# One planned order for attention and experts: other planned landing times for transfers, and one due-time shift per operation

## The chip, the cores and the metric

The kernel runs on one core of a Trainium2 chip. The metric is the device time of one execution in microseconds (us), less is better. TensorE is called PE here, VectorE DVE, ScalarE ACT, GpSimd POOL and SyncE SP. Each engine works through its own list of instructions in the order in which the program issued them; an instruction that waits holds up everything behind it on its engine.

## The reference, cut to what matters

```python
scores = scale * q @ k.T                       # 8 batches x 8 heads, 576 x 576, head size 64
thresh = max(scores, axis=-1) - tau
scores = where(scores >= thresh, scores, -1e9)
attn = softmax(scores);  x = attn @ v          # x as 4608 tokens x 512
e_idx = argmax(x @ w_gate + modality_bias[modality_id])      # one of 8 experts per token
h = relu(x[mask] @ w1[e]);  out[mask] = gate_w * (h @ w2[e]) # 512 -> 1024 -> 512
```

## The kernel before

**Attention** goes through 32 pairs of heads (4 pairs to a batch) with 9 steps each, 288 steps in all. A step is: scores on PE (line 819, into one of two score buffers `s`), negated row maximum on DVE (828), exponential on ACT (834), mask and sum on DVE (846, into `pr`), four transposes of `pr` on PE (872) and their copy on ACT (875). The rest of each score row goes through `rp` (copied on POOL in the first 54 steps, line 859; transposed on PE at 885 and 889). After a pair come the products with v (753, `ptm` and `ptr`). Ahead of a pair its q and k rows are loaded into the single buffer `kq` by SP (line 482), transposed on PE (684 and 690), copied on ACT, and split by POOL into `q` (719, 721), from which SP copies `km`, `nk` and `q` halves.

**Experts.** When a batch's four pairs are done, `gate` (966, 976) and `route` work out each token's expert and place: the transposes at 976, a chain on DVE that ends in `oh` (1009), the counting matmuls on `oh` (printed with line 753), again DVE, and five scatters into the table `tab` (POOL, 1038). Eight side slots, one for each batch, take up to 512 routed tokens each: SP reads the slot's list `tb` from `tab` (1156), POOL gathers its tokens' rows `xg` (1165), PE transposes them (1182), weights come through `raw` (1198, 1203) and are split by POOL (1216, 1218), PE computes both layers (1234 and 1266) with ACT and DVE between them (1246 `hh`, 1248 `hl`), and POOL scatters the result (1285). What is left is worked out by `pick_rest` on DVE (from 1065) after the last attention step and done in a tail.

**What sets the order.** Nothing is issued as written: each `op(...)` is recorded with a cost and a due time, and `Plan.order` plays the program through with these costs, always starting the waiting operation that is due first on a free engine. A transfer is given an issue time, a share of a common transfer queue and a landing time; a consumer is not placed before its input has landed in this play. The order that comes out is fixed at build time. Where the play leaves PE free for over 0.6, `Plan.fill` puts small matmuls of zeros there (line 1430, here called fillers), which do nothing but keep PE at work. Before the play each operation's due time is shifted: in the kernel before by some 900 entries `(seed, lo, hi, wide)`, each of which adds Gaussian noise of width `wide` to all operations due between `lo` and `hi`.

Of the kernel before, what the change touches and what calls it, by code (L numbers as in the profile page):

```python
# [76 lines left out]
class Plan:  # L77
# [65 lines left out]
    def order(self, banks, late):  # L143
# [43 lines left out]
        dma = [0.0]  # L187
# [10 lines left out]
        def begin(e, t):  # L198
# [3 lines left out]
            for j in coming:  # L202
                x = ops[j]
# [35 lines left out]
            if o.dma is not None:  # L239
                s = max(dma[0], end + (0.9 if t > self.COLD else 0.0))  # L240
                dma[0] = s + 1.15 * o.dma
                fin = dma[0] + (2.6 if t > self.COLD else 1.2)
                if e == "POOL":
                    fin = max(fin, end + 3.7)
                    sent.append(fin)
            else:
                fin = end
# [94 lines left out]
def tile_attn_moe(  # L342
# [19 lines left out]
    N = B * S  # L362
# [1066 lines left out]
    def idle(g, n):  # L1429
# [3 lines left out]
    SHIFTS = [  # L1433
# [180 lines left out]
```

## Time and profile before

| | us |
|---|---|
| median of 3 runs | 1006.26 (1003.15 to 1007.72) |
| profiled execution | 999.88 |
| its span, from the first instruction to the last | 998.1 |
| PE busy in the span | 969.2 (97%) |
| DVE busy | 738.6 (74%) |
| ACT busy | 616.6 (62%) |
| POOL busy | 562.8 (56%) |
| mean granted clock of PE | 0.996 of full |

The profiled execution lies 6.4 us below the median of the runs, and 1.8 us of it lie outside the span. Busy time is the union of an engine's instructions; PE's matmuls overlap, and a filler counts as busy.

### The profile page before, as it was taken

To read this page: it belongs to the slowest core of one execution; us is meant where nothing else is said; L and a number is where in the kernel's file an instruction comes from. 1 tells how busy PE (TensorE), PEld (TensorE's weight loads), DVE (VectorE), ACT (ScalarE), POOL (GpSimd) and SP (SyncE) were. 2 spreads that over 40 slices of the span, in tenths; PEclk is the share of its full clock that TensorE was granted. 3 is DMA by queue.
4 is the path that set the end of the run, shared out by engine and by line. 5 is a ranking of instruction groups with operands and counts; after the bars stand their busy time and mean duration, and the time that the engine had idled before them with its cause. 6 is when DMAs were issued, how large, how long until landed. Compare 5 with 4: busy or idle time off the path is not lost.

```text
span 998.1 us, 20124 instructions
## 1 busy us (share of the span) xinstructions
PE 969.2 (97%) x6527; PEld 782.4 (78%) x6527; DVE 738.6 (74%) x1802; ACT 616.6 (62%) x1256; POOL 562.8 (56%) x693
## 2 busy tenths in 40 slices
PE   7989989999999999999999999999999999999997
PEld 6667678777888877888888778877887778888886
DVE  7889878898888888888988888878886373233341
ACT  6677667777777767777677667765775213243431
POOL 5433577475557652756666564646854679933341
PEclk9999999999999999999999999999999999999999
DMA  8787798789969975789689786987662258443421
GB/s 173 132 188 176 159 191 197 157 175 192 187 121 196 208 185 101 161 183 210 159 160 238 168 179 100 211 170 165 142 178 86 66 149 265 137 125 102 121 81 40
DMA packets 291122, 158.10 MB, mean 158 GB/s; under 512 B 199038, under 2 KB 262526, under 8 KB 289088
## 3 DMA queue, kind: packets, MB, share of 16 engines
q1 hardware_dynamic: 281696, 137.28, 63.0%
q0 software_dynamic: 7200, 18.92, 6.3%
q8 instruction: 54, 0.88, 0.4%
q10 hardware_dynamic: 2112, 0.52, 0.3%
q14 instruction: 60, 0.49, 0.2%
HBM read 85.83 MB, written 19.35 MB: 105 GB/s over the span
## 4 chain that ended last, share of the span: by engine, by line
PE 85%; DVE 5%; issue 3%; DMA 3%; ACT 1%; POOL 1%; SPq 0%; DVEq 0%; POOLq 0%; ACTq 0%
PE s L819 16%; PE bk L1266 16%; PE bk L753 15%; PE bk L1234 14%; PE bk L872 11%; PE pm L1234 3%; PE pm L1266 2%; PE bk L1182 1%; PE bk L941 1%; PE bk L885 1%; DMA tab<-pay,posi 1%; PE bk L966 1%; DVE nm L828 1%; DVE pr L846 1%; ACT e L834 1%
## 5 line engine op out<-in xcount | busy, mean ns | idle before, releaser
L828 DVE TENSOR_REDUCE nm<-s 128x1 f32<-128x576 f32 x288 | 216.4, 752 | 61.9 <-PE s L819 59.4
L834 ACT ACTIVATE e<-s,nm 128x576 f32<-128x576 f32 x288 | 213.5, 745 | 64.6 <-DVE nm L828 59.3
L846 DVE SCALAR_TENSOR_TENSOR pr<-s,nm,e 128x576 f32<-128x576 f32 x288 | 231.8, 812 | 25.7 <-ACT e L834 14.2
L819 PE MATMUL s<-km,q 128*128 128x288 f32 x1024 | 189.0, 310 | 2.9 <-DVE pr L846 2.7
L875 ACT COPY ptm<-bk 128x512 f32<-128x512 f32 x256 | 147.9, 588 | 57.8 <-PE bk L872 52.0
L819 PEld LDWEIGHTS s<-km,q 128*128 128x128 f32 x1024 | 146.9, 189 | 30.1 <-DVE pr L846 12.4
L872 PE MATMUL bk<-ident,pr 128*128 128x128 f32 x1152 | 168.8, 273 | 1.0 <-ACT kqt L687 1.0
L872 PEld LDWEIGHTS bk<-ident,pr 128*128 128x128 f32 x1152 | 137.3, 140 | 19.0 <-issue 3.3
L753 PE MATMUL bk<-ptm,v_m 128*64 128x320 f32 (+1 forms) x1024 | 137.8, 412 | 0.2
L753 PEld LDWEIGHTS bk<-ptm,v_m 128*64 128x64 f32 x1024 | 68.2, 136 | 48.8 <-issue 8.3
L1234 PE MATMUL bk<-xh,w1h 128*128 128x512 f32 (+2 forms) x244 | 92.6, 379 | 0.0
L1266 PE MATMUL bk<-w2h,hh 128*128 128x512 f32 x204 | 88.0, 431 | 3.0 <-DVE hl L1248 2.8
L721 POOL TENSOR_TENSOR q<-kqt,q 128x576 fp32r<-128x576 f32 x62 | 88.2, 1423 | 4.0
L1218 POOL TENSOR_TENSOR w1l<-raw,w1h 128x512 fp32r<-128x512 f32 x64 | 82.8, 1294 | 4.4
L1234 PE MATMUL bk<-xh,w1l 128*128 128x512 f32 (+2 forms) x244 | 85.2, 349 | 0.0
L1234 PE MATMUL bk<-xl,w1h 128*128 128x512 f32 (+2 forms) x244 | 85.1, 349 | 0.0
L1218 POOL TENSOR_TENSOR w2l<-raw,w2h 128x512 fp32r<-128x512 f32 x64 | 82.0, 1283 | 4.5
L719 POOL CAST q<-kqt 128x576 fp32r<-128x576 f32 x62 | 41.1, 665 | 72.7 <-PE s L819 54.9
L1266 PE MATMUL bk<-w2h,hl 128*128 128x512 f32 x204 | 80.9, 397 | 0.0
L1266 PE MATMUL bk<-w2l,hh 128*128 128x512 f32 x204 | 80.8, 396 | 0.0
L1216 POOL CAST w1h<-raw 128x512 fp32r<-128x512 f32 x64 | 39.6, 619 | 67.0 <-PE bk L1234 58.0
L1246 ACT ACTIVATE hh<-bk 128x512 fp32r<-128x512 f32 (+3 forms) x74 | 38.6, 521 | 58.8 <-PE bk L1234 58.1
(232 smaller groups left out, 1780.3 us busy)
## 6 DMA issues: line engine op xcount, KB each, us to landing
raw<-in_moe_w_dram SPq DMA_DIRECT2D x128, 256.0 KB, 4.0
km<-q SPq DMA_DIRECT2D x60, 288.0 KB, 4.4
q<-q SPq DMA_DIRECT2D x30, 576.0 KB, 5.1
nk<-km SPq DMA_DIRECT2D x97, 144.0 KB, 3.8
traw<-in_moe_w_dram SPq DMA_DIRECT2D x48, 256.0 KB, 3.0
v_m<-in_v_dram SPq DMA_DIRECT2D x64, 128.0 KB, 3.3
xs<-xr SPq DMA_DIRECT2D x32, 256.0 KB, 3.1
kq<-in_q_dram SPq DMA_DIRECT2D x46, 144.0 KB, 3.7
```

The lines of the kernel that those rows point to most:

```text
L719: op("POOL", 0.665, lambda s=s: nc.gpsimd.tensor_copy(out=q2[:, 0, s], in_=kqt[:, s]), [kqt[:, s]], [q2[:, 0, s]])
L721: op("POOL", 1.5, lambda s=s: nc.gpsimd.tensor_tensor(out=q2[:, 1, s], in0=kqt[:, s], in1=f32(q2[:, 0, s]), op=ALU.subtract), [kqt[:, s], ...
L753: nc.tensor.matmul(out=o, lhsT=lhsT, rhs=rhs, start=start, stop=stop, skip_group_check=True)
L819: nc.tensor.matmul(out=g.t[:, hf, 0:SH], lhsT=a, rhs=x, start=(z == 0), stop=(z == len(passes) - 1))
L828: op("DVE", 0.753, lambda: nc.vector.tensor_reduce(out=nm[:, 0, x:x + 1], in_=g.t[:, :, 0:SH], axis=AX.XY, op=ALU.max, negate=True), [g], ...
L834: op("ACT", 0.747, lambda: nc.scalar.activation(out=e, in_=g.t[:, :, 0:SH], func=AF.Exp, bias=nm[:, 0, x:x + 1]), [g, nm[:, 0, x:x + 1]], ...
L846: op("DVE", 0.88, lambda: nc.vector.scalar_tensor_tensor(out=pr.rearrange("p (a x) -> p a x", a=2), in0=g.t[:, :, 0:SH], scalar=nm[:, 1, x ...
L872: op("PE", 0.44, lambda: [nc.tensor.transpose(out=g.t[:, kc * P:(kc + 1) * P], in_=pr[:, kc * P:(kc + 1) * P], identity=ident) for kc in r ...
L875: op("ACT", 0.583, lambda: nc.scalar.copy(out=o, in_=g.t.rearrange("a (k p) -> a k p", p=P)), [g], [o])
L1218: op("DVE" if d else "POOL", 0.902 if d else 1.37, lambda: (nc.vector if d else nc.gpsimd).tensor_tensor(out=lo.t, in0=raw.t, in1=f32(hi.t ...
L1234: nc.tensor.matmul(out=g.t[:, 0:WT], lhsT=a.t[:, cs], rhs=x.t[:, c, 0:WT], start=(c == 0 and y == 0), stop=(c == KC - 1 and y == 2))
L1266: nc.tensor.matmul(out=g.t, lhsT=a.t[:, ts], rhs=w.t, start=(y == 0 and i == 0), stop=(y == F2 - 1 and i == 2))
```

## The change

Two things change, both ahead of the issue of any instruction. First the play's figures for transfers. Second the shifts: in place of the list of seeds there is a string with two characters for each of the 5751 recorded operations, which are read as one shift of its due time in hundredths. No operation is added, removed or changed; the matmuls that compute are the same in number, and the fillers are 99 where they were 119.

```diff
             if o.dma is not None:
-                s = max(dma[0], end + (0.9 if t > self.COLD else 0.0))
-                dma[0] = s + 1.15 * o.dma
-                fin = dma[0] + (2.6 if t > self.COLD else 1.2)
+                s = max(dma[0], end + (0.5 if t > self.COLD else 0.0))
+                dma[0] = s + 1.07 * o.dma
+                fin = dma[0] + (1.9 if t > self.COLD else 1.2)
                 if e == "POOL":
-                    fin = max(fin, end + 3.7)
+                    fin = max(fin, end + 4.7 - o.dma)
                     sent.append(fin)
...
-    SHIFTS = [
-        (515427, 173, 233, 0.3), (614633, 760, 820, 3), (985271, 408, 558, 0.1), (531926, 381, 406, 0.3),
...
-    base = [o.due for o in plan.ops]
-    for seed, lo, hi, wide in SHIFTS:
-        draw = random.Random(seed)
-        for o, d in zip(plan.ops, base):
-            if lo <= d < hi:
-                o.due += draw.gauss(0, wide)
+    SHIFTS = (
+        'PPPPPPPPPPPPPPPPMXPPPPPPPPPPQ/PPPPPPPPPPPPPPQDR0N`PmMbPSPPPPPPPPPPPPSyPPPPPPPPPEPBPbP?PBPkWvLBVMP?Z}'
...
+    digit = {c: i for i, c in enumerate(c for c in map(chr, range(35, 127)) if c != chr(92))}
+    assert len(SHIFTS) == 2 * len(plan.ops)
+    for o, x, y in zip(plan.ops, SHIFTS[0::2], SHIFTS[1::2]):
+        o.due = o.due + (91 * digit[x] + digit[y] - 4140) / 100
```

With a free transfer queue, and counted from the start of the issue, the play's landing times go from 4.81 to 3.66 for a 144 KB load of `kq`, from 5.19 to 4.01 for a 256 KB load of `raw`, from 5.01 to 5.78 for a scatter into `tab` and from 5.95 to 5.00 for a gather of `xg`. These are figures of the play.

Three places show what this moves. The first is PE at steps 25 to 30 (third and fourth pair of heads); the rows with `kq` are the transposes of a later pair's q and k rows. Before:

```order
L819 MATMUL s1_76<-km0_164,q20_162 128x288 x4
L872 MATMUL bk2_79<-ident_126,pr2_180 128x128 x4
L872 MATMUL bk1_78<-ident_126,pr1_179 128x128 x4
L684 MATMUL bk0_77<-ident_126,kq_160 128x128 x4
L684 MATMUL bk3_80<-ident_126,kq_160 128x128 x4
L819 MATMUL s0_75<-km0_164,q20_162 128x288 x4
L872 MATMUL bk2_79<-ident_126,pr3_181 128x128 x4
L819 MATMUL s1_76<-nk_166,qb0_167 128x288 x6
```

and in the changed kernel, from the same scores of step 25 on:

```order
L819 MATMUL s1_76<-km0_164,q20_162 128x288 x4
L941 MATMUL bk2_79<-ident_126,ot1_188 128x128 x4
L872 MATMUL bk3_80<-ident_126,pr2_180 128x128 x4
L684 MATMUL bk1_78<-ident_126,kq_160 128x128 x4
L684 MATMUL bk0_77<-ident_126,kq_160 128x128 x4
L753 MATMUL bk2_79<-ptm0_0_182,v_m0_171 64x256 x4
L819 MATMUL s0_75<-km0_164,q20_162 128x288 x4
...
L819 MATMUL s1_76<-km1_165,q21_163 128x288 x4
L872 MATMUL bk1_78<-ident_126,pr2_180 128x128 x4
L889 MATMUL bk3_80<-ident_126,rp_186 128x128
L684 MATMUL bk0_77<-ident_126,kq_160 128x128 x4
L885 MATMUL bk1_78<-ident_126,rp_186 128x128 x4
```

Two `kq` transposes stand together ahead of step 26 in both kernels, but they are not the same two. The list has 16 of them, two for each of the pairs that are loaded by rows. Before, the two here are the eighth and the ninth, and the ninth is the first of the next pair, whose loads come later. In the changed kernel they are the seventh and the eighth, and the ninth stands only after step 29.

The second place is POOL ahead of the second side slot's gathers (`xg` by the list `tb1`), from the first slot's store of results (`out_0_dram`) on. Before:

```order
L1285 DMA out_0_dram<-y0_117,tb0_119 4608x512
L1218 TENSOR_TENSOR w1l1_89<-raw2_83,w1h1_86 128x512
L1216 CAST w2h0_91<-raw0_81 128x512
L1216 CAST w2h1_92<-raw1_82 128x512
L1218 TENSOR_TENSOR w2l0_95<-raw0_81,w2h0_91 128x512
L1218 TENSOR_TENSOR w2l1_96<-raw1_82,w2h1_92 128x512
L1165 DMA xg0_99<-xs_142,tb1_120 128x512
L1165 DMA xg2_101<-xs_142,tb1_120 128x512
```

and in the changed kernel:

```order
L1218 TENSOR_TENSOR w1l1_89<-raw2_83,w1h1_86 128x512
L1285 DMA out_0_dram<-y0_117,tb0_119 4608x512
L1165 DMA xg0_99<-xs_142,tb1_120 128x512
L1165 DMA xg1_100<-xs_142,tb1_120 128x512
L1216 CAST w2h1_92<-raw1_82 128x512
L1218 TENSOR_TENSOR w2l1_96<-raw1_82,w2h1_92 128x512
L1165 DMA xg2_101<-xs_142,tb1_120 128x512
L719 CAST q21_163<-kqt_161 128x576
```

Between the store and the first gather stood five splits of weights; now nothing stands there. On PE, ahead of the transposes of these rows, there were two groups of fillers (17 and 20), and there is one (19).

The third place is DVE where `pick_rest` begins (`left`, `done`, `th`), with the differences `hl` of the last side slot. Before:

```order
L1060 CAST pk_i7_159<-pk1_150 1x2
L1065 TENSOR_TENSOR left_9311<-pos1_146,nxt_147 1x8
L1067 TENSOR_TENSOR done_9313<-nxt_147,creg_130 1x8
L1248 SCALAR_TENSOR_TENSOR hl0_109<-bk0_77,hh0_105 128x512
L1072 SCALAR_TENSOR_TENSOR th_9325<-th_lo_131,left_9311 1x72 x3
L1248 SCALAR_TENSOR_TENSOR hl1_110<-bk2_79,hh1_106 128x512
```

and in the changed kernel:

```order
L1060 CAST pk_i7_159<-pk1_150 1x2
L1248 SCALAR_TENSOR_TENSOR hl0_109<-bk2_79,hh0_105 128x512
L1065 TENSOR_TENSOR left_9290<-pos1_146,nxt_147 1x8
L1067 TENSOR_TENSOR done_9292<-nxt_147,creg_130 1x8
L1072 SCALAR_TENSOR_TENSOR th_9305<-th_lo_131,left_9290 1x72 x2
L1248 SCALAR_TENSOR_TENSOR hl1_110<-bk3_80,hh1_106 128x512
```

The first `hl` moved ahead of `left`, and one of the three `th` behind the second `hl`; the second `hl` is still behind `left`.

## Rows read from the trace of the kernel before

**Rows 1.** The page: busy us (share of the span) xinstructions.

```profile
PE 969.2 (97%) x6527; PEld 782.4 (78%) x6527; DVE 738.6 (74%) x1802; ACT 616.6 (62%) x1256; POOL 562.8 (56%) x693
```

**Rows 2.** Windows: stretch, length, busy of PE, PEld, DVE, ACT, POOL, clock, DMA.

```profile
0.00:250.00 250.00, 232.65 (x1811) 182.74 (x1812) 210.70 (x544) 174.83 (x347) 134.25 (x220) 1.00 0.83 174
250.00:790.00 540.00, 537.64 (x3799) 435.79 (x3798) 448.44 (x1126) 375.48 (x793) 316.15 (x352) 1.00 0.75 165
790.00:830.00 40.00, 37.53 (x167) 30.40 (x166) 21.15 (x53) 9.78 (x17) 33.02 (x38) 0.96 0.57 152
...
985.00:998.10 13.10, 6.72 (x29) 5.10 (x28) 2.37 (x4) 0.00 (x0) 2.90 (x3) 0.86 0.15 51
```

**Rows 3.** Waits of PE, whole run: us in total, times, longest.

```profile
PE bk L684 <- DMA kq<-in_q_dram: 3.9, 3, 2.5
...
PE bk L1266 <- DVE hl L1248: 2.8, 2, 2.5
PE bk L1182 <- DMA xg<-xs,tb: 2.2, 1, 2.2
PE bk L885 <- POOL rp L859: 1.8, 1, 1.8
```

**Rows 4.** Timeline of PE near 62 us: start, length, [idle before and its releaser].

```profile
64.59 0.63 PE L684 MATMUL bk<-ident,kq 128*128 128x128 f32 x4 [2.53 <-DMA kq<-in_q_dram]
```

**Rows 5.** Timeline of POOL near 220 us.

```profile
216.25 1.01 POOL L1285 DMA_INDIRECT out_dram<-y,tb  x1 [0.22 <-DVE nm L830]
...
222.31 1.06 POOL L1165 DMA_INDIRECT xg<-xs,tb  x1 [0.16 <-issue]
```

**Rows 6.** The chain that ended last near 222 us: start, length, what.

```profile
222.31 5.70 DMA xg<-xs,tb
```

**Rows 7.** Windows of the fillers (line 1430) alone: PE and PEld busy.

```profile
0.00:250.00 250.00, 7.97 (x119) 7.15 (x119) 1.00 0.83 174
...
220.00:230.00 10.00, 2.39 (x37) 2.23 (x37) 1.00 1.00 238
```

**Rows 8.** Timeline of DVE where `pick_rest` begins.

```profile
803.55 0.15 DVE L1065 TENSOR_TENSOR left<-pos,nxt 1x8 f32<-1x8 f32 x1 [15.94 <-DMA tab<-pay,posi]
...
803.71 0.67 DVE L1248 SCALAR_TENSOR_TENSOR hl<-bk,hh 128x512 fp32r<-128x512 f32 x1
804.31 1.57 DVE L1072 SCALAR_TENSOR_TENSOR th<-th_lo,left 1x72 f32<-1x72 f32 x3
805.81 0.67 DVE L1248 SCALAR_TENSOR_TENSOR hl<-bk,hh 128x512 fp32r<-128x512 f32 x1
```

**Rows 9.** The chain: second-layer matmuls right after that place, and later.

```profile
806.54 6.67 PE bk L1266 x21
...
839.26 3.02 PE bk L1266 x12
```

**Rows 10.** Windows at that place.

```profile
805.00:810.00 5.00, 3.46 (x9) 2.72 (x10) 4.79 (x19) 0.00 (x0) 4.23 (x6) 0.67 0.76 210
```

**Rows 11.** The chain in the first batch's routing on PE.

```profile
105.71 0.87 PE bk L872 x8
106.58 1.01 PE bk L753 x8
...
109.35 0.27 PE bk L690 x2
109.62 0.25 PE bk L753 x6
```

**Rows 12.** DMA issues: xcount, KB each, median us from issue to landing.

```profile
raw<-in_moe_w_dram SPq DMA_DIRECT2D x128, 256.0 KB, 4.0
...
kq<-in_q_dram SPq DMA_DIRECT2D x46, 144.0 KB, 3.7
...
tab<-pay,posi POOLq DMA_INDIRECT x40, 6.7
```

**Rows 13.** The instructions of tile `xg`: its transfers' landing.

```profile
DMA to landing us min/median/max: 2.3/5.4/7.3
```

116 lines of the change are left out of this document (115 added, 1 removed), and 119 rows, old and new, of the table SHIFTS.

## Prediction

> **What bounds the kernel now.** The page comes first: PE is busy for 969.2 us of a span of 998.1, and no other engine for more than 738.6 [rows 1]. Order can't take anything off that work, only the idle time around it and the fillers in it. So the next question is where PE is idle, and the windows say it [rows 2]: 250.00 - 232.65 = 17.4 us in the first 250, 2.4 us in the 540 us after that, 2.5 us between 790 and 830, and 6.4 us in the last 13 (of 998.1 - 969.2 = 28.9 in all, so next to nothing is left for the rest). The last 13 us are the end of the tail, whose last matmuls, results and store stand in the same order in both kernels; I take nothing from there. The fillers count as busy, and all 119 of them lie in the first 250 us, with 7.97 us [rows 7]. What an order can win is therefore at most 17.4 + 8.0 in the first quarter, and some 5 us in all behind it.
>
> The waits of PE tell what the idle time waits for [rows 3]. Most are small and many; four single ones stand out: 2.5 us for a load of `kq`, 2.2 for gathered rows `xg`, 2.5 for the differences `hl`, 1.8 for `rp`. The rest of the idle time in the first quarter is spread over short waits for the chain of the softmax, on a DVE that is busy for 210.7 of the 250 us [rows 2].
>
> **The change, part by part.** The engines do the same operations for the same time, so each term is a wait or fillers that go or come. I go through the places in order of time and set the sum against the profiled execution, 999.88 us.
>
> *The ninth `kq` transposes.* The ninth set of these transposes stands right behind the eighth and starts at 64.59 us, after a wait of 2.53 for its load [rows 4]. In the changed kernel the ninth stands some four steps later, behind their scores and transposes, while its loads are issued at about the same place of SP's list. All 288 steps are done before `left` starts at 803.55 [rows 8], so one takes some 2.8 us, and the load lands behind work that must be done anyhow. The whole wait would be -2.5; if PE only waits for something else instead (the `pr` of DVE), 0. I take **-2.3**, since three or more steps now cover it.
>
> *The copy of `rp` on POOL.* PE waits 1.8 us for it once [rows 3]. In the changed kernel POOL has two gathers ahead of the copy that it feeds; a gather holds POOL for 1.06 us [rows 5], so the copy could also come later. Bounds: -1.8 (gone), and +2.5 (two gathers of 1.06 and the gaps between). With causes both ways I take **0**.
>
> *The second slot's gathers.* The first slot's store on POOL ends at 216.25 + 1.01 = 217.26, and the first gather starts at 222.31 [rows 5]; the 5.05 us between are the five splits that the change moves behind it. The gathered rows land 5.70 us after the start [rows 6], and PE waits 2.2 us for them [rows 3], after 37 fillers that cost 2.39 us [rows 7]. The gather can start up to 5 us sooner; the wait then goes, and there are 19 fillers in place of 37: 18 x 2.39 / 37 = 1.2. So -2.2 - 1.2 = **-3.4**. At best all fillers there were dear too, 2.2 + 2.39 = -4.6; at worst 0, if the splits that now come later hold up the slot's weights, or the transposes have moved ahead as far as the rows have. The splits are needed only by the first layer's matmuls, which stand some way behind the transposes, and that is why I take the middle term.
>
> *`hl` and `pick_rest`.* On DVE `left` waits 15.94 us for the scatters into `tab` and starts at 803.55; behind it stand the first `hl`, three `th` and the second `hl`, which ends at 805.81 + 0.67 = 806.48 [rows 8], and PE waits 2.5 us for it [rows 3]. In the changed kernel the first `hl` (0.67, of which 0.6 are its own between 803.71 and 804.31) is done before the scatters land, and one `th` (1.57 / 3 = 0.5) comes later: PE is released 1.1 us sooner. Behind the wait stands a second loss: the clock is 0.67 in the window there [rows 10], and the 21 matmuls behind it take 6.67 us, where later ones take 3.02 for 12 [rows 9], so 6.67 - 21 x 3.02 / 12 = 1.4 more. At 62 us PE waited as long, and the clock of that stretch is 1.00 [rows 2, 4]; so a shorter wait may keep the clock or may not, and I count half, 0.7. Together **-1.8**; bounds 0 (the scatters land later by as much) and -2.5 - 1.4 = -3.9.
>
> *The first batch's routing.* DVE works out `oh` between the transposes at 976 and the counting matmuls. Before, PE has work from 105.71 to 109.62, 3.9 us, between the two [rows 11]. In the changed kernel's order there stand only four transposes of `pr`, two of `kq`, eight matmuls with v and six fillers: 0.87 / 2 + 0.27 + 1.01 [rows 11] + 6 x 7.97 / 119 [rows 7] = 2.1. DVE's chain has not become shorter, so PE waits up to 3.9 - 2.1 = 1.8 where it did not. DVE may get to that chain sooner by as much as it has less beside it; the fillers stand there because the play sees a gap too. I take **+1.4**, from 0 to +1.8.
>
> *The landing times.* The play now reckons 4.01 for a load of `raw` and 3.66 for one of `kq`, where 4.0 and 3.7 are measured [rows 12]; the old figures were over 1 us longer. A consumer is thus put about where its input lands, with no reserve. For the scatters the play goes from 5.01 to 5.78 with 6.7 measured [rows 12], which is nearer; for the gathers from 5.95 to 5.00, where the median is 5.4 and the longest 7.3 [rows 13], which is farther off on the short side. PE's transposes of `xg` are then in line 0.4 us too soon at the median. With eight slots that is 3 us, but most slots have their rows long ahead of the need, as one wait for `xg` in the whole run shows [rows 3]. I take **+0.6**, as for one or two slots; bounds 0 and 8 x (7.3 - 5.0) = +18.
>
> That transfers don't all take the same time has a row: from 2.3 to 7.3 us for gathers of the same kind [rows 13], in a kernel whose transfer engines are busy for 0.75 to 0.83 of the time [rows 2]. The Trainium skill, "DMA: Bandwidth & Descriptors", section "Latency and other measured facts", says that a transfer's fixed cost is mostly the access latency of HBM, 0.2 us on average and 2 us at high load. By that rule a plan with a short fixed part is wrong just where the traffic is dense, and as an estimate from that page 2 us on each of eight slots would be +16 in place of +0.6. The trace agrees in that the spread is there; that PE waits for it in each slot no row shows.
>
> The sum is -2.3 + 0 - 3.4 - 1.8 + 1.4 + 0.6 = -5.5, so 994.4 for an execution like the profiled one. That one lies 6.4 us under the median of its runs; the same difference on the median gives 1006.26 - 5.5 = **1000.8**.
>
> **The rivals.** *Waits change places.* The early stretch is paced by DVE's softmax, and PE, let through at one place, waits for `pr` at the next. For it speaks that DVE is busy for 210.7 of the first 250 us while PE is idle for 17.4 of them [rows 2]; against it, that DVE still has 39 us free there, and that the wait at 804 us lies outside. The terms at 62 and 222 us vanish, -1.8 + 1.4 + 0.6 remain: 1006.
>
> *Much more of the early idle time goes.* With a shift for each operation, and figures nearer to the measured ones for most loads, many small waits could go, not only the four that I can point to. For it: 17.4 us idle and 8.0 of fillers in that stretch [rows 2, 7], and loads that no longer keep a reserve of over 1 us. Against it: the slots' beginnings, the steps and the fillers' number (99) have moved little. Half of 25.4 would be 12.7: 1006.3 - 12.7 = 993.6.
>
> *The gathers come too late for their place.* PE's transposes of `xg` stand right where the play lets rows land, 5.00 after the issue; where they take 7.3 [rows 13], PE waits 2.3 with all that is behind it, scores too. Without the +0.6 the other terms give -6.1; for a loss of 0.5%, or 5 us, the slots must lose 11.1 us in all, 1.4 in each of the eight. At 1.5 each: 1006.3 - 6.1 + 12.0 = 1012.2. Against it: one slot of eight waits now [rows 3], and POOL, where the splits lie that a gather must pass, has over a third of its time free [rows 1].
>
> **How the numbers follow.** I give my forecast 0.45, the places' exchange 0.25, the larger gain 0.20, the late gathers 0.10. About 0.5% or 5 us is what a measurement of this kernel can tell from no change, and the bound for faster is 1001.2, just above the forecast; of its own range, 996 to 1004, I put two thirds on the faster side (0.31). Faster: 0.31 + 0.20 = 0.51; the same: 0.14 + 0.25 = 0.39; slower: 0.10. The range reaches from the middle of the larger gain and somewhat beyond, 990, to 1009, above the exchange and below the late gathers; it leaves out the farther third of the gain and most of the late gathers, 0.15 or so.
>
> **What would show it.** Right: no wait over 1 us for `kq` near 62 us and none for `xg` near 222; the wait for `hl` under 1.6 us, at whatever clock behind it; a new wait for `oh` of up to 1.8 near 107; PE idle in the first 250 us down from 17.4 to 12 or 13. Wrong: the idle time of that stretch as before with longer waits for `pr` (exchange), or below 9 (larger gain), or waits for `xg` in four or more slots (late gathers). I could also be wrong outside all of this, if the matmuls between 250 and 985 us take another time: there PE is idle for under 3 us, and only its busy time could move.

## The result and the profile after

The changed kernel is slower: 1012.60 us (median of 4 runs, 1012.09 to 1013.67) against 1005.87 for the kernel before (4 runs), a ratio of 1.0070 [1.0045, 1.0096]. On another occasion it took 1007.72 (12 runs) against 1003.74 (20 runs), 1.0037 [1.0020, 1.0054]; why it took 5 us less there is open. The forecast was 1000.8, so its sign was wrong, and 1012.6 lies above its range too. The execution profiled after the change took 1012.93, with a span of 1011.1; before it was 999.88 with 998.1, which is less than any of its four runs. The spans are 13.0 us apart, of which some 6 belong to that quick execution.

The page after (compare [rows 1]), and the windows by stretch (columns as in [rows 2]):

```profile
PE 972.4 (96%) x6507; PEld 786.1 (78%) x6507; DVE 734.8 (73%) x1802; ACT 619.7 (61%) x1256; POOL 563.9 (56%) x693
```

```profile
0.00:150.00 150.00, 129.03 (x998) 99.16 (x998) 120.68 (x313) 98.12 (x183) 69.34 (x146) 0.98 0.80 162
150.00:250.00 100.00, 93.86 (x712) 75.57 (x711) 79.77 (x205) 67.41 (x145) 59.92 (x67) 0.98 0.78 168
250.00:790.00 540.00, 536.15 (x3781) 437.20 (x3782) 451.42 (x1125) 384.11 (x804) 314.44 (x350) 1.00 0.77 166
790.00:830.00 40.00, 39.40 (x210) 30.33 (x207) 19.73 (x67) 9.62 (x18) 28.28 (x32) 1.00 0.38 94
```

The same first stretch in the kernel before:

```profile
0.00:150.00 150.00, 136.35 (x1072) 103.79 (x1073) 125.19 (x330) 103.40 (x195) 72.97 (x150) 1.00 0.80 170
```

PE's idle time is 38.7 us where it was 28.9, 9.8 more. Of this, 129.03 against 136.35 puts 7.3 into the first 150 us; the next 100 give 2.4 (6.1 idle, before 17.35 - 13.65 = 3.7), the stretch to 790 gives 1.5, and the one from 790 to 830 takes back 1.9. PE's busy time grew by another 3.2 us for the same computing matmuls. The clock is enough to explain that:

```profile
140.00:145.00 5.00, 4.42 (x23) 3.75 (x24) 1.79 (x4) 3.50 (x8) 4.84 (x7) 0.59 1.01 249
145.00:150.00 5.00, 4.95 (x27) 3.69 (x25) 3.52 (x8) 3.61 (x9) 2.23 (x3) 0.73 1.07 131
240.00:245.00 5.00, 5.00 (x29) 4.33 (x30) 4.23 (x12) 3.91 (x9) 4.81 (x6) 0.67 1.22 151
335.00:340.00 5.00, 5.00 (x28) 4.72 (x27) 3.03 (x5) 1.52 (x5) 4.46 (x5) 0.66 1.19 219
```

A granted clock between half (1.2 GHz) and full (2.4 GHz) in a 5 us window costs about 5 x (1 - clock): 3.4, 1.65 and 1.7 us here, 6.75 in all, against 1.65 in the one such window of [rows 10], which is gone.

What PE waits for now (compare [rows 3]):

```profile
PE s L819 <- DVE pr L846: 7.3, 10, 2.0
PE s L819 <- issue: 4.7, 3, 3.5
PE bk L885 <- POOL rp L859: 2.6, 1, 2.6
PE bk L753 <- DVE oh L1009: 2.1, 3, 0.9
PE bk L1182 <- DMA xg<-xs,tb: 2.1, 1, 2.1
```

The single long waits have moved, and none of the old ones is simply gone except that for `hl`. In the order of time, on PE:

```profile
53.18 0.80 PE L819 MATMUL s<-km,q 128*128 128x288 f32 x4 [1.57 <-DVE pr L846]
...
73.60 0.63 PE L684 MATMUL bk<-ident,kq 128*128 128x128 f32 x4 [1.62 <-DMA kq<-in_k_dram]
...
118.38 0.80 PE L819 MATMUL s<-km,q 128*128 128x288 f32 x4 [1.99 <-DVE pr L846]
...
140.10 0.33 PE L885 MATMUL bk<-ident,rp 128*128 128x128 f32 x1 [2.55 <-POOL rp L859]
...
238.50 0.77 PE L819 MATMUL s<-km,q 128*128 128x288 f32 x4 [3.52 <-issue]
...
334.69 0.63 PE L1182 MATMUL bk<-ident,xg 128*128 128x128 f32 x4 [2.13 <-DMA xg<-xs,tb]
```

Half clock follows the waits at 140, 238 and 334. A mark that all orders share is the last of the 288 row maxima on DVE (line 828). Before and after it starts at

```profile
764.08 0.76 DVE L828 TENSOR_REDUCE nm<-s 128x1 f32<-128x576 f32 x1 [0.35 <-PE s L819]
```

```profile
780.33 0.76 DVE L828 TENSOR_REDUCE nm<-s 128x1 f32<-128x576 f32 x1 [0.35 <-PE s L819]
```

that is 16.2 us later, while what follows is shorter: 1011.1 - 780.33 = 230.8 against 998.1 - 764.08 = 234.0. The play, in its own figures, has this row maximum at 753.6 before and at 754.4 after. For the play the two orders are the same up to there; the chip falls 10.5 us behind the play with the first and 25.9 with the second. Starts of some row maxima, counted on DVE:

| row maximum no. | 21 | 43 | 61 | 97 | 149 | 288 |
|---|---|---|---|---|---|---|
| before | 53.1 | 99.8 | 146.0 | 243.8 | 383.7 | 764.1 |
| after | 55.6 | 103.0 | 154.6 | 255.9 | 399.5 | 780.3 |
| after, the other occasion (h3 below) | 56.1 | 103.1 | 154.2 | 255.4 | 397.5 | 775.9 |

At no. 61 the changed kernel is 8.6 us behind the kernel before, of 16.2 at no. 288; in h3 it is 8.2 of 11.9. More than half of the lag is thus there after the first 150 us.

### The profile page after: what moved, and what is told of

It reads as the page before. It is cut to its first block, busy times and chain, and to the rows that moved or that the text cites. A ratio compares the mean times of both kernels' runs of the same rounds, so it can differ in the third digit from the quotient of the medians.

```text
span 1011.1 us, 20037 instructions
## 1 busy us (share of the span) xinstructions
PE 972.4 (96%) x6507; PEld 786.1 (78%) x6507; DVE 734.8 (73%) x1802; ACT 619.7 (61%) x1256; POOL 563.9 (56%) x693
## 4 chain that ended last, share of the span: by engine, by line
PE 80%; DMA 5%; DVE 4%; issue 3%; POOL 3%; SPq 2%; ACT 1%; POOLq 0%; DVEq 0%; ACTq 0%
PE bk L1234 17%; PE s L819 15%; PE bk L1266 14%; PE bk L753 13%; PE bk L872 10%; PE pm L1266 3%; SPq L482 2%; PE bk L1182 1%; PE bk L941 1%; PE pm L1234 1%; PE bk L885 1%; DVE nm L828 1%; DMA qb<-q 1%; PE bk L966 1%; DMA km<-q 1%
## 5 line engine op out<-in xcount | busy, mean ns | idle before, releaser
L819 PE MATMUL s<-km,q 128*128 128x288 f32 x1024 | 191.9, 313 | 12.5 <-DVE pr L846 6.8
L875 ACT COPY ptm<-bk 128x512 f32<-128x512 f32 x256 | 147.7, 588 | 65.1 <-PE bk L872 57.6
L753 PE MATMUL bk<-ptm,v_m 128*64 128x256 f32 (+1 forms) x1024 | 137.2, 412 | 0.1
L1234 PE MATMUL bk<-xh,w1h 128*128 128x512 f32 (+2 forms) x252 | 95.5, 379 | 0.0
L1248 DVE SCALAR_TENSOR_TENSOR hl<-bk,hh 128x512 fp32r<-128x512 f32 (+3 forms) x81 | 47.9, 593 | 56.5 <-ACT hh L1246 55.6
L1234 PE MATMUL bk<-xh,w1l 128*128 128x512 f32 (+2 forms) x252 | 88.3, 350 | 0.0
L1234 PE MATMUL bk<-xl,w1h 128*128 128x512 f32 (+2 forms) x252 | 88.1, 350 | 0.0
L1266 PE MATMUL bk<-w2h,hh 128*128 128x512 f32 x196 | 83.3, 425 | 0.0
L1266 PE MATMUL bk<-w2l,hh 128*128 128x512 f32 x196 | 77.2, 394 | 0.7 <-POOL w2l L1218 0.7
L1266 PE MATMUL bk<-w2h,hl 128*128 128x512 f32 x196 | 77.4, 395 | 0.0
L861 ACT COPY rp<-pr 128x64 f32<-128x64 f32 x234 | 55.9, 249 | 31.2 <-DVE pr L846 28.1
```

The lines of the kernel that those rows point to most:

```text
L753: nc.tensor.matmul(out=o, lhsT=lhsT, rhs=rhs, start=start, stop=stop, skip_group_check=True)
L819: nc.tensor.matmul(out=g.t[:, hf, 0:SH], lhsT=a, rhs=x, start=(z == 0), stop=(z == len(passes) - 1))
L861: op("ACT", 0.248, lambda: nc.scalar.copy(out=o, in_=i), [i], [o])
L875: op("ACT", 0.583, lambda: nc.scalar.copy(out=o, in_=g.t.rearrange("a (k p) -> a k p", p=P)), [g], [o])
L1234: nc.tensor.matmul(out=g.t[:, 0:WT], lhsT=a.t[:, cs], rhs=x.t[:, c, 0:WT], start=(c == 0 and y == 0), stop=(c == KC - 1 and y == 2))
L1266: nc.tensor.matmul(out=g.t, lhsT=a.t[:, ts], rhs=w.t, start=(y == 0 and i == 0), stop=(y == F2 - 1 and i == 2))
```

## The experiments

**Which half of the change.** One kernel has the table with the old figures, one the seeds with the new figures, two have no shifts at all, with the new and with the old figures. In the form of a diff against the changed kernel, e1 is

```diff
-                s = max(dma[0], end + (0.5 if t > self.COLD else 0.0))
-                dma[0] = s + 1.07 * o.dma
-                fin = dma[0] + (1.9 if t > self.COLD else 1.2)
+                s = max(dma[0], end + (0.9 if t > self.COLD else 0.0))
+                dma[0] = s + 1.15 * o.dma
+                fin = dma[0] + (2.6 if t > self.COLD else 1.2)
                 if e == "POOL":
-                    fin = max(fin, end + 4.7 - o.dma)
+                    fin = max(fin, end + 3.7)
```

and e2 is the same edit the other way round in the kernel before; e3 and e4 drop the shifts.

> Old transfer figures (0.9, 1.15, 2.6, 3.7), new table. Theory 1 (the shorter figures put consumers right where a transfer lands, so they wait in line): most of the 6.7 us loss goes, 1004 to 1008. Theory 2 (the table makes the bad order, whatever the figures): still about 1012, 1010 to 1015. Theory 3 (a table or list fits only the figures that it was found with): above the changed kernel, 1014 to 1022.

> New transfer figures, the list of seeds of before. Theory 1 (figures): slow like the changed kernel, 1010 to 1015, with new waits of PE for transfers. Theory 2 (table): as before, 1003 to 1008. Theory 3 (fit of shifts to figures): slower than the changed kernel, 1014 to 1022.

> New figures, no shifts at all. What the figures alone are worth, beside the run with the old figures and no shifts. Theory 1: slower than that run by 5 us or more. Theory 2: within 4 us of it. Theory 3: within 4 us of it, and both at 1014 or more, since the shifts are what makes either order good; the table is then worth what this run lies above 1012.6.

> Old figures, no shifts at all. Theory 1: faster than the run with the new figures and no shifts by 5 us or more. Theories 2 and 3: within 4 us of it. What it lies above 1005.9 is what the seeds are worth with their own figures; I expect 8 to 25 us.

| | old figures | new figures |
|---|---|---|
| no shifts | 1022.67, 1.0169 [1.0147, 1.0192] | 1023.10, 1.0160 [1.0139, 1.0181] |
| seeds | before: 1006.47 | 1027.25, 1.0211 [1.0192, 1.0229] |
| table | 1014.66, 1.0074 [1.0053, 1.0096] | after: 1.0037 and 1.0070 |

Without shifts, the figures change nothing in the whole run (1.0169 and 1.0160). The seeds gain 16 us with the figures that they stand beside in the kernel before, and lose 4 with the others: they have their worth with one set of figures. The table gains 8 us with the old figures and 9 to 12 with its own, so for the table this is not shown; with its own figures it gains less than the seeds with theirs. That leaves the question of where the table's order loses.

For the first 150 us the traces of these four kernels answer it. The start of row maximum no. 61, one profile each:

| | old figures | new figures |
|---|---|---|
| no shifts | 149.3 | 153.1 |
| seeds | before: 146.0 | 154.9 |
| table | 147.7 | after: 154.6 |

With each list of shifts it comes later with the new figures, by 3.8, 8.9 and 6.9 us; with the table and the old figures it is only 1.7 later than before. Over all twenty profiles of this document it starts at 144.5 to 149.3 in the nine with the old figures in that stretch, and at 153.1 to 158.4 in the eleven with the new ones. So it is the figures that make the beginning slow, and not the table. One wait that goes with it is that of a cast on POOL (`qb`, line 741) for the copies into `q`. In the first 150 us, in total, times and longest, before, after, e1 and e2:

```profile
POOL qb L741 <- DMA q<-q: 0.6, 1, 0.6
```

```profile
POOL qb L741 <- DMA q<-q: 7.6, 5, 3.9
POOL qb L741 <- DMA vr<-in_v_dram: 3.4, 1, 3.4
```

```profile
POOL qb L741 <- DMA q<-q: 2.2, 2, 2.0
```

```profile
POOL qb L741 <- DMA q<-q: 11.3, 4, 3.8
```

The copies of `rp` and the splits into `q` stand behind that cast on POOL. It is not the whole account: without shifts the wait is 2.3 with the old figures and 3.6 with the new. And e1 doesn't keep what it has at no. 61: from there to the last row maximum it takes 634 us, where the kernel before takes 618 and the changed one 626 (its profiled execution is the slowest of its six).

**Repairing single waits.** The order is a list of operations; these kernels take operations out of the finished list and put them back elsewhere, with all else the same:

```diff
-        for i in plan.fill(plan.order(4, marks["close"]), 4, idle):
+        todo = plan.fill(plan.order(4, marks["close"]), 4, idle)
+        for i, j in ((700, 882), (714, 700), (854, 714),):
+            todo.remove(i)
+            todo.insert(todo.index(j) + 1, i)
...
+        for i in todo:
```

This is f1, which brings the `rp` copy of 140 us ahead of the gathers on POOL. The others differ in the pairs: f2 `(1336, 1565)` issues the copy into `q` that is waited for at 238 us sooner; f3 has both and `(2088, 2130), (2089, 2088), (2090, 2089)`, which puts the transposes of the rows `xg` waited for at 334 us behind more work; f4 is `(5085, 5041), (5088, 5055)` in the kernel before, which gives its DVE the new order of `hl` and `pick_rest` and nothing else.

> The changed kernel, with one edit of the finished order: on POOL the copy of rp that PE waits 2.55 us for at 140 us stands ahead of the first slot's two gathers and of the nk cast, instead of behind them. Theory A (the 13 us are single places where a planned time was missed, and they add up): the wait and most of the half clock behind it go, -3.0 to -5.0, 1007.6 to 1009.6. Theory B (the order is tight everywhere, and what goes at one place is waited for at the next): less than a third of it, 1011.5 or more.

> The changed kernel, with one edit of the finished order: on SP the 576 KB copy of q that PE waits 3.5 us for at 238 us is issued four loads sooner, behind the first of three loads of raw; some 3 us. Theory A: the wait and the half clock behind it go, -3.0 to -4.5, 1008.1 to 1009.6. Theory B: 1011.5 or more.

> The changed kernel with three edits of the finished order: the two others of this batch, and on PE the first transposes of the third slot's gathered rows (a wait of 2.1 us at 334 us) behind the next ten score matmuls, with their copy on ACT and difference on DVE. Theory A: the sum, -9 to -13, so 1000 to 1004, below the kernel before. Theory B: 1009 or more.

> The kernel before, with one edit of the finished order, the one that the prediction costs at 804 us: on DVE the first hl ahead of left and done, and one th behind the second hl. By the prediction's term -1.8 (between -1.1, the shorter wait alone, and -3.9, wait and half clock gone): 1004.4 against about 1006.2. If the term is nothing because the scatters land later: 1006.

Measured: f1 1009.38, 1.0062 [1.0039, 1.0085]; f2 1007.93, 1.0042 [1.0019, 1.0064]; f3 1007.86, 1.0033 [1.0014, 1.0052]; f4 1004.74, 1.0004 [0.9983, 1.0025]; the kernel before beside them 1003.24. f1 and f2 lie between the two results of the changed kernel itself and f3 is 0.0004 below them, so no gain is shown for any; f3 was to bring 9 to 13 us. In f1 PE still waits at the repaired place, as a copy of `q` is late next:

```profile
135.63 0.76 PE L819 MATMUL s<-km,q 128*128 128x288 f32 x4 [1.96 <-DMA q<-q]
...
142.58 0.33 PE L889 MATMUL bk<-ident,rp 128*128 128x128 f32 x1 [2.05 <-POOL rp L859]
```

f4 is the prediction's `hl` term alone, and no gain is shown for it; -1.8 lies at the edge of its interval, which goes from -1.7 to +2.5 us. The place itself does what was expected: the second `hl` starts 38.9 us behind the last row maximum in place of 41.7, and PE's wait of 2.5 for it is gone. But in the profiled execution, the slowest of its twelve, some of DVE's small operations (33 to 264 elements) are held further on, and PE waits longer for the next `hl`:

```profile
807.28 0.15 DVE L1065 TENSOR_TENSOR left<-pos,nxt 1x8 f32<-1x8 f32 x1 [2.72 <-DMA tab<-pay,posi]
...
817.72 3.64 DVE L1112 TENSOR_TENSOR bj<-bj,ij 1x33 f32<-1x33 f32 x1
...
823.92 0.67 DVE L1248 SCALAR_TENSOR_TENSOR hl<-bk,hh 128x512 fp32r<-128x512 f32 x1
```

```profile
824.65 0.79 PE L1266 MATMUL pm<-w2h,hl 128*128 128x512 f32 x1 [4.11 <-DVE hl L1248]
```

That wait is not the move's: g4 below, which has the old order there, has it too, with 3.8.

**A place that I had not seen.** Row maximum 21 is already 2.5 us late. On DVE of the changed kernel, the work on the modality bias (lines 638 to 646) stands ahead of a row maximum that is due:

```profile
47.70 0.18 DVE L638 CAST y<-xg 128x40 f32<-128x40 int32 x1 [0.80 <-DMA xg<-in_moe_modality_id_dram]
...
48.55 1.64 DVE L643 TENSOR_TENSOR bias_t<-xg,y 128x320 f32<-128x320 f32 x1
...
50.63 0.75 DVE L828 TENSOR_REDUCE nm<-s 128x1 f32<-128x576 f32 x1
```

Before, it stands behind two of them:

```profile
45.08 0.76 DVE L828 TENSOR_REDUCE nm<-s 128x1 f32<-128x576 f32 x1
...
46.04 0.76 DVE L828 TENSOR_REDUCE nm<-s 128x1 f32<-128x576 f32 x1
...
47.94 0.17 DVE L638 CAST y<-xg 128x40 f32<-128x40 int32 x1
```

PE waits 1.57 at 53.18 for the `pr` that comes of it. With the same kind of edit, g1 `(242, 344), (247, 242), ...` puts the bias behind the row maxima in the changed kernel; g2 `(729, 853)` brings a `q` copy sooner at 122 us; g3 has both, the `q` copy of f2 and the `xg` transposes of f3; g4 `(242, 305), (244, 242), ...` puts the fault into the kernel before.

> The changed kernel, with one edit of the finished order: the five DVE instructions that set up the bias (638 to 646, they wait for loads of the modality ids at 47 us) stand behind the two row maxima of the next scores, as in the kernel before, instead of ahead of them. Theory A (single places where an input lands later than planned and a whole engine waits behind its consumer; they add up): -2 to -4, a ratio of 1.003 to 1.005 to the kernel before where the changed kernel has 1.007. Theory B (the order is tight everywhere, what goes here is waited for later): 1.006 or more.

> The changed kernel, with one edit of the finished order: on SP the 576 KB copy of q that POOL's qb cast waits 3.4 us for at 135 us, with both rp copies behind it, is issued ahead of five kq loads, some 4 us sooner. Theory A: POOL's line moves up, the wait for rp at 140 us (2.55 and 0.48) and the half clock behind it go, -2.5 to -5, a ratio of 1.002 to 1.0045. Theory B: the kq loads are late instead, 1.006 or more.

> The changed kernel with four edits of the finished order: the two others of this batch, the copy of q at 229 us sooner on SP, and the first transposes of the third slot's gathered rows behind ten score matmuls. Theory A: the sum, -8 to -13, a ratio of 0.994 to 0.999, at or below the kernel before. Theory B: 1.004 or more.

> The kernel before, with one edit of the finished order, the fault of the changed kernel put in: the five DVE instructions of the bias ahead of the two row maxima. Theory A: +2 to +4, a ratio of 1.002 to 1.004. Theory B, or if the place has nothing to do with it: 1.000 within 0.002.

Measured: g1 1012.91, 1.0086 [1.0067, 1.0106]; g2 1007.72, 1.0038 [1.0018, 1.0059]; g3 1007.23, 1.0052 [1.0030, 1.0073]; g4 1005.46, 1.0022 [1.0006, 1.0039]. The fault costs 2.2 us where it is put in (0.6 to 3.9 by the interval), but taking it out gives nothing. Nor do g2 and g3: both stay between the changed kernel's two results, and g3 was to bring 8 to 13 us. In g1 row maximum 21 is at 54.6 in place of 55.6, and no. 33 at 82.8 in place of 80.9, since PE then waits 1.72 for an `rp` and 1.82 for a load of `kq` behind it:

```profile
72.29 0.33 PE L889 MATMUL bk<-ident,rp 128*128 128x128 f32 x1 [1.72 <-POOL rp L859]
...
74.44 1.09 PE L684 MATMUL bk<-ident,kq 128*128 128x128 f32 x4 [1.82 <-DMA kq<-in_k_dram]
```

**Less traffic, the change again, and a split.** h1 (from before) and h2 (from after) load a quarter of the weights of most slots and of the rows of v from the third pair on:

```diff
-            load(t[:, s], sv[s, 0:SA, :].rearrange("(c p) d -> p c d", c=NC), us=0.6)
+            c_ = 1 if p > 1 else NC
+            load(t[:, s, 0:c_], sv[s, 0:c_ * P, :].rearrange("(c p) d -> p c d", c=c_), wr=[t[:, s]], us=0.6)
...
-                            out=raw.t.rearrange("p (o a f) -> p o a f", o=1, a=KC),
+                            out=raw.t.rearrange("p (o a f) -> p o a f", o=1, a=KC)[:, :, 0:part(KC)],
```

h3 is the changed kernel once more. h4 is the kernel before with figures and table of the changed one only where the play (for the figures) or the due time (for the table) is past 735 us, that is, for the last of the attention and the tail:

```diff
-                s = max(dma[0], end + (0.9 if t > self.COLD else 0.0))
-                dma[0] = s + 1.15 * o.dma
-                fin = dma[0] + (2.6 if t > self.COLD else 1.2)
+                p = ((0.9, 1.15, 2.6) if t < 735 else (0.5, 1.07, 1.9))
+                s = max(dma[0], end + (p[0] if t > self.COLD else 0.0))
+                dma[0] = s + p[1] * o.dma
+                fin = dma[0] + (p[2] if t > self.COLD else 1.2)
                 if e == "POOL":
-                    fin = max(fin, end + 3.7)
+                    fin = max(fin, end + (3.7 if t < 735 else 4.7 - o.dma))
...
+    for o, d, x, y in zip(plan.ops, base, TABLE[0::2], TABLE[1::2]):
+        if d >= 735:
+            o.due = d + (91 * digit[x] + digit[y] - 4140) / 100
```

i1 and i2 are the same edit with 150 and 270 in place of 735.

> The order of the kernel before, but with three quarters of the bytes of most loads of weights (raw) and of v left out, on the stale rest of the buffers; the values are then wrong, the instructions and their order are the same. Theory C (the changed order is slower because its transfers land later than its play reckons): this kernel gains little, 0 to 4 us, since its waits for transfers are few. Theory D (the waits of the changed order are waits for engines, whatever the transfers): the same. It is here for the difference to the next run.

> The changed kernel with the same three quarters of the loads of weights and of v left out. Theory C: it gains 5 us or more, and lies within 3 us of the run before it in this batch. Theory D: it gains no more than that one, and stays 5 to 9 us above it.

> The changed kernel once more, on the chip of this batch, for the comparison with the repaired orders: 1.007 to the kernel before. If it is 1.004 here, the single repairs have done nothing, by theory B; if 1.007 or more, the copies of q that were issued sooner were worth some 3 us each in the median.

> A join of the two orders: the kernel before's seeds and figures up to 735 in the play, the table and the new figures after that; its order is that of before to the end of the attention steps, nearly, and that of the changed kernel in the tail. From the last step's row maximum to the end the profiles show 230 to 231.5 us in the orders with the changed tail and 234 to 237 in the three with the tail of before. If that holds: -3 to -6, a ratio of 0.994 to 0.997, faster than both. If the tail's length depends on what comes ahead of it: 1.000 within 0.002.

> The join of the two orders with the border at 150 in the play: seeds and old figures ahead of it, table and new figures behind it. The play makes it 980.2 long, as long as the others. Theory F (most of the loss lies ahead of 150, where the changed order is 9 to 10 us behind at step 60, and 2 to 3 of it behind): the tail's -5 and +2 to +3, so -2 to -3, a ratio of 0.997 to 0.998. Theory G (the new figures and the table cost the same everywhere in the attention steps, 11 us over 764): +9 in 610 us of steps and -5, a ratio of 1.004.

> The same with the border at 270 in the play (its play is 978.5 long). Theory F: as the join at 735, with +2 at 334 us if the third slot's wait comes back: 0.994 to 0.996. Theory G: +7 in 490 us of steps and -5, a ratio of 1.002.

h1 took 1086.30 and h2 1086.74. With other values of v the tokens go to other experts and the tail grows, so these times say nothing; the attention part does. The last row maximum, in h1 and h2:

```profile
761.02 0.76 DVE L831 TENSOR_REDUCE nm<-s 128x1 f32<-128x576 f32 x1 [0.36 <-PE s L822]
```

```profile
773.05 0.76 DVE L831 TENSOR_REDUCE nm<-s 128x1 f32<-128x576 f32 x1 [0.35 <-PE s L822]
```

12.0 us apart, against 16.2 in the full kernels and 775.93 - 764.08 = 11.9 with h3. The traffic of the first 250 us had gone from 174 GB/s [rows 2] to 154 in h1, but that of the first 150 only from 170 to 162. A cut of that size doesn't close the gap.

h3 gave the 1.0037 quoted above. h4 took **997.33**, 0.9932 [0.9911, 0.9953]; i1 1002.69, 0.9955 [0.9935, 0.9974] (one execution of its ten took 3347.78 and is not in the interval); i2 1002.27, 0.9965 [0.9952, 0.9977], both against 1005.96. So the changed figures and table are an improvement with each of the three borders tried, and a loss only with the first 150 us of the play in them: from 0.9955 to 1.0037 or 1.0070 is 0.8 to 1.15%, 8 to 12 us. Between 150 and 735 us no gain is shown: h4, which leaves that stretch out, is no slower than i1 and i2. In i1 the first stretch is that of the kernel before:

```profile
0.00:150.00 150.00, 136.94 (x1070) 103.84 (x1071) 125.25 (x330) 103.34 (x195) 72.88 (x150) 1.00 0.80 169
```

and in h3 that of the changed kernel:

```profile
0.00:150.00 150.00, 130.82 (x1000) 100.87 (x1001) 121.20 (x314) 97.97 (x183) 69.23 (x146) 0.97 0.80 162
```

Between them lie 6.1 us of idle time, and a clock of 0.97 on 150 us for some 4.5 more; row maximum no. 61 is 154.2 - 146.1 = 8.1 us apart. h4 is faster than both kernels. Its gain is behind the last row maximum: that starts at 766.9, no sooner than in the two other profiles whose attention part is nearly the same order (765.7 in g4, 769.3 in f4), and 229.9 us follow it, where 234.0 did in [rows 1]'s execution, 236.6 in f4 and 237.4 in g4. In all eleven profiles with the changed tail and all of the traffic it is 229.9 to 231.5. What in the tail's order does this, no run tells.

## Why the prediction was wrong

The sum was -5.5. For the tail its sign is right (-1.8; the profiles give -3.2 and h4 -6.4), in part by luck, since the move that was priced is not shown to be the cause. The rest has the wrong sign: the first 150 us, for which it held three terms (-2.3 + 0 + 1.4 = -0.9) and a share of the landing times, cost 7.3 of idle time and 3.4 of clock in the profiled execution. The step that failed is the term for the landing times, +0.6: what the shorter figures do in those 150 us is 7 to 9 us with either list of shifts. The terms in the prediction's order:

*The ninth `kq` transposes (-2.3).* The wait of [rows 4] is gone, but it comes back at 73.60 with 1.62. The statement that failed is "its loads are issued at about the same place of SP's list". SP before and after:

```profile
60.37 1.24 SPq L482 DMA_DIRECT2D kq<-in_k_dram  x2
61.66 0.51 SPq L482 DMA_DIRECT2D kq<-in_q_dram  x1
```

```profile
67.84 2.51 SPq L482 DMA_DIRECT2D kq<-in_q_dram  x2
70.40 0.50 SPq L482 DMA_DIRECT2D kq<-in_k_dram  x1
...
224.62 0.41 SPq L1156 DMA_DIRECT2D tb<-tab  x1
...
229.54 0.52 SPq L482 DMA_DIRECT2D q<-q  x1
```

The loads went later with the transposes, the last by 70.40 - 61.66 = 8.7 of the 9.0 us between 64.59 and 73.60. In nine profiles of this order and its repairs the wait was 0.8 to 2.6. Instead of -2.3 the move is worth about -0.9 in this pair of executions (2.53 - 1.62), and less in others: where the old order was profiled again, the wait was 0 (g4) to 2.4 (f4), so the 2.53 that was priced is the longest that it showed.

*The copy of `rp` (0, bound +2.5).* The bad end came: 2.55 in place of 1.8, and half clock behind it for 3.4 us. On POOL:

```profile
134.71 0.29 POOL L741 CAST qb<-q 64x128 fp32r<-64x128 f32 x1 [3.40 <-DMA vr<-in_v_dram]
...
136.78 1.08 POOL L1165 DMA_INDIRECT xg<-xs,tb  x1 [0.99 <-DMA tb<-tab]
138.17 1.02 POOL L1165 DMA_INDIRECT xg<-xs,tb  x1 [0.31 <-issue]
...
139.81 0.24 POOL L859 COPY rp<-pr 128x64 f32<-128x64 f32 x1
...
222.87 1.00 POOL L1285 DMA_INDIRECT out_dram<-y,tb  x1 [1.08 <-DVE y L1278]
228.71 1.06 POOL L1165 DMA_INDIRECT xg<-xs,tb  x1 [4.84 <-DMA raw<-in_moe_w_dram]
```

The two gathers that I counted are there, but the larger part is in front of them: a cast that reads a copy into `q` stands on POOL with nothing that could go first, and waits 3.40 (the timeline names another transfer; in f1 the same cast waits for `q<-q`), then a gather waits for its list. The prediction asks what POOL does ahead of `rp`, and not what POOL itself waits for. The move of `rp` alone (f1) does not bring the time back.

*The second slot's gathers (-3.4).* The wait for `xg` near 222 is gone and 19 fillers are there, as forecast. "The gather can start up to 5 us sooner" failed: it starts at 228.71, 5.84 after the start of the store at 222.87, where 6.06 were between them [rows 5]. Now POOL waits there 4.84 instead of splitting weights, for the list `tb`, whose load SP issued at 224.62, behind the store (at 215.56, ahead of it, in the kernel before). (The timeline names `raw`; the list was issued 4.1 us ahead of the gather's start, and nothing else that the gather needs was.) Then PE waits 3.52 at 238.50 for the copy into `q` that SP issued at 229.54, and half clock follows. The term is not -3.4: one wait of 2.2 and 1.2 of fillers went, and 3.5 with 1.65 of clock came, +1.8 in all at this place. That PE waited for this copy is inferred from the POOL cast behind it; the trace names no releaser, and f2, which issues it sooner, stays within the changed kernel's two results.

*`hl` and `pick_rest` (-1.8).* The wait of 2.5 is gone, and so is the low clock of [rows 10]. But for the move that was priced no gain is shown by itself (f4, 1.0004). The part of the order from 735 us on, as a whole, is worth 6.4 us (h4).

*The first batch's routing (+1.4).* About right in size: a wait of 0.92 for `oh` stands at 108.91, and the `pr` behind it are late, by 1.99 at 118.38. By the row maxima this stretch (no. 43 to 49) took 17.5 us before and 19.1 to 20.9 in the profiles of the changed order. In the whole run the waits for `oh` did not grow (2.1 in three, 2.8 in four before).

*The landing times (+0.6).* Here the prediction has the right idea ("A consumer is thus put about where its input lands, with no reserve") and prices it by the gathers alone. The loads and copies of q and k in the first 150 us, whose landing times went down with the same figures, it puts at nothing, without a reason. The runs showed in its place 6.9 us (table) and 8.9 us (seeds) at row maximum no. 61, and waits of POOL's `qb` cast for copies into `q` of 8.8 to 13.4 us in the nine profiles of the changed order, where the old one has 0 to 0.7. Of the gathers, one slot waits as before, now the third: 2.13 at 334.69, and half clock costs 1.7 behind it; h3 has the wait with 2.4, i1 with 1.0. That part is nearer to 2 or 3 us than to 0.6, and far from the +12.0 of the late-gathers rival. The spread that was read from [rows 13] is too wide: the rows hold small loads into the same tile as well, and 2.3 is one of these; the gathers alone have 5.6 at the median and none below 3.4.

*What was left out.* The bias on DVE at 47.70 is in none of the terms, and it costs 2.2 us where it was put in alone. The prediction prices the waits of the old order, and the places of the new one that it names; it does not search the first 150 us of the new order for operations that now stand ahead of a row maximum or a scores matmul and have an input that lands late. And its premise "The engines do the same operations for the same time" failed: matmuls at half clock take longer, and the bias product took 1.64 in place of 0.49 (see the last section). The sentence that failed as a whole is "What an order can win is therefore at most 17.4 + 8.0": it takes the idle time as a ceiling of gains only. It has no ceiling for losses, and a planner that sees 753.6 and 754.4 for two orders 16 us apart on the chip gives none.

In number the late gathers came nearest (1012.2), by luck: one slot waits, not eight. In mechanism "waits change places" was the nearest, and it was 4 to 7 us short (1006 against 1006.26 x 1.0037 = 1010.0 and x 1.0070 = 1013.3), since the waits came back longer and dropped the clock. Settled by runs: that the loss needs what the first 150 us of the play hold (h4, i1, i2 against h3), that without shifts the figures are worth nothing in the whole run (e3, e4), and that no repair of single waits shows a gain, alone or together (f1 to f3, g1 to g3). Shown by one profile each of e1 to e4, and by all others in line with them: that in those 150 us the figures cause the lag. Open stays how the 8 to 12 us divide among the many small waits there, and why the table with the old figures falls behind later. Traffic was excluded only for the cut that was tried.

## What to carry to other kernels

Shifts can be worth something only beside the figures that they were found with: the seeds gained 16 us with theirs and lost 4 with the others. Planned landing times near the measured median leave less reserve for a transfer that lands later, and here the shorter ones cost 7 to 9 us in the first 150. When rows move, look for each moved operation at what its own engine waits for just ahead of it, also on engines that are far from busy, and don't price the removal of a wait before the next operation's input is known to be there. When a planner's change wins in one stretch and loses in another, split it at a time of the plan: of the three such kernels here one (h4) is 0.7% faster than the kernel before.

## What the runs showed of the hardware that I had not expected

A half clock followed PE's waits of 2.13 to 3.52 us at 140, 238 and 334 us of the changed kernel, but not that of 2.53 at 64.59 before [rows 2, 4].

Small DVE operations take far longer when POOL works beside them: the 33-element one of f4 above took 3.64 us where the same one took 0.18 before, and the bias product 1.64 in the changed kernel where it took 0.49 before (at 48.77). POOL beside the first (f4) and beside the second (after):

```profile
818.49 2.53 POOL L1218 TENSOR_TENSOR w1l<-raw,w1h 128x512 fp32r<-128x512 f32 x2
```

```profile
48.43 1.41 POOL L721 TENSOR_TENSOR q<-kqt,q 128x576 fp32r<-128x576 f32 x1
```

Both DVE operations end some 0.35 us behind POOL's. In all seven profiles in which that product of POOL lies beside the bias product, the latter took 1.63 or 1.64; beside a cast of POOL it took 0.88 (e3), and in the twelve with nothing on POOL beside it 0.48 or 0.49. The row maximum, which reads the scores where PE wrote them, doesn't show this: 751 ns on average in the changed kernel, where POOL is busy for 56% of the span.

In the changed kernel's first profile PE had done scores and transposes by 115.4 and went on to 17 fillers, but the row maximum that waits for PE started only at 116.83, after 1.76 of idle time; PE then waited 1.99 for its `pr`, at 118.38. Other profiles of this order do not show this.

The issue of a load on SP is not even either: in the changed kernel the 70 issues of `kq` loads from `in_q_dram` took 338 to 3739 ns, 597 at the median, and what stands behind one on SP waits for it.
